# The last product of an FFN by a 7-for-8 algorithm, one factor of the weight at a time, on one Trainium2 core

## The chip, the core and the metric

The kernel runs on one core of a Trainium2 chip. Its engines have queues of their own and run side by side: TensorE (PE) multiplies 128-row tiles into PSUM banks, VectorE (DVE) and ScalarE (ACT) work on PSUM and SBUF, GpSimd (POOL) on SBUF, and SyncE (SP) issues all DMAs of this kernel. The metric is the time of one execution on the device in microseconds; lower is better.

## The reference

Attention over 8 batches, 12 heads, 448 tokens and head size 64, with q and k normalized, and then an FFN without activation: two products of the 3584 x 768 attention output with 768 x 1536 weights, multiplied elementwise, and a last product with a 1536 x 768 weight. The weights come as float64.

```python
q_n, k_n = (rmsnorm(q, g_q), rmsnorm(k, g_k))
scores = scale * np.matmul(q_n, k_n.transpose(0, 1, 3, 2))
attn = softmax(scores)                       # rows
x = np.matmul(attn, v) -> (3584, 768)
out = ((x @ w_a) * (x @ w_b) @ w_out).astype(np.float32)
```

## The kernel before

**Order by a planner.** Nearly every operation is given to a small planner, class Plan, with its engine, an estimated duration, a key, and what it reads and writes. The planner goes forward in estimated time; on each engine it takes, of the operations that could start first, the one with the smallest key. The order that it finds is written out: each engine then works through its list in that order, and waits in it. Durations on the chip don't change the order.

**Attention** runs over 48 pairs of heads (`p` = 0 to 47; six pairs per batch). Per pair: load q, k, v; squares, `ms` sums, a power on POOL (L428); `qn` (L432); transposes on TensorE (L461) and their copies to `qkT` (L466 on ACT, L470 on DVE); scores (L483) and exponentials (L489, ACT) in four chunks; the product with v (L504); sums over keys (L539), from the fourteenth pair on over chunks first added up on DVE and POOL (L517, L519); reciprocals (L557); the result to `x` (L574, L578). The first 12 pairs (`LEAD`) use another split among engines.

**The FFN** runs in four blocks (`beta` = 0 to 3) of two batches, 896 tokens, once their 12 pairs are through. Its operations have larger keys than attention's, so on TensorE it fills what attention leaves. The first two products (`quarter_products`, L657) already use an algorithm with 7 products in place of 8: 12 steps per block, each with one "factor" tile `st` of 7 sums of weight quarters, into two of the PSUM banks "mm", evacuated on DVE, ACT and POOL into `hT`; the evacuation `U` (L685, L687) is an early one of each step. Input tiles `x` are nine, of which a block uses seven, so attention can run ahead of a block by one batch only, and stands still until its products are through.

**The last product** (L625) is plain: 7 chunks of 128 tokens, 2 halves of 384 columns, 12 matmuls each with all of w_out in SBUF (`w_out_sb`), copied from PSUM on DVE (L635) and ACT (L637) and stored.

**The weights** are rounded from float64 in 36 pieces of 128 x 768: one operation on ACT (L258), five on DVE (L259, L260, L262, L264, L265), one on POOL (L267). For w_a and w_b, two pieces make a factor (three sums on DVE, one on POOL, L343), which is kept in DRAM (L349) for blocks 1 to 3 and loaded again there (`stream`). Three `st` buffers rotate over factors in the making and in use. The 12 pieces of w_out (`round_out`) go to `w_out_sb`, the first eight through the memory of `hT`, the last four through `st` buffers.

## Time and profile before

| | |
|---|---|
| time, median of 3 runs | 1730.97 us (1730.71 to 1731.92) |
| profiled execution | 1732.12 us, its span 1730.2 us |
| TensorE busy | 1650.3 us, 95% |
| DVE busy | 742.7 us, 43% |
| POOL, ACT busy | 543.1 us, 372.2 us |
| moved by DMA | 139.49 MB |

The profile is of one execution. Busy time is that in which an engine has at least one instruction at work. The rows of a group give line, engine, operation and shapes, count, busy us and mean ns of one, and behind the bar the idle time just before them. The rows of waits give who waited for whom, us in total, times and the longest. Rows of the timeline give start, duration, engine, line, count, and in brackets the idle time before and what ended it. Rows of windows give a stretch and the busy us and count of each engine in it.

### The profile page before, as it was taken

Reading aid. Unit: us, or ns where it says so; the run is one execution under the profiler, and the core shown is the slowest. Engines: PE = TensorE matmul, PEld = TensorE weight load, DVE = VectorE, ACT = ScalarE, POOL = GpSimd, SP = SyncE. Lnnn points to the kernel's source line nnn. Section 1 sums busy time; section 2 is a strip of 40 time slices with the busy share of each in tenths; the row PEclk is TensorE's granted clock in tenths of the full one; section 3 lists DMA queues with packets and bytes.
Section 4 is the critical chain, followed back from the end, with each engine's and each line's share of the span. In section 5 each row is a group of like instructions: output and inputs, shape, how many; then the busy total and the mean of one; then the engine's idle time right before and its main releaser. Section 6 shows DMA issues by size and latency. Waiting matters only on the chain. (4 is left out here: it accounts for less than half of the span.)

```text
span 1730.2 us, 14844 instructions
## 1 busy us (share of the span) xinstructions
PE 1650.3 (95%) x5616; PEld 803.3 (46%) x5616; DVE 742.7 (43%) x936; ACT 372.2 (22%) x666; POOL 543.1 (31%) x320
## 2 busy tenths in 40 slices
PE   5799799899889999999999999999999999999998
PEld 2333343344344444555444544455544555555554
DVE  8877687876644434222353534222253202222100
ACT  5676223221222223000132223100023000000000
POOL 4535556553544445010164444201042000010000
PEclk9899899999989999999999999999999999999999
DMA  8343133443331111222221111222220001220000
GB/s 285 110 119 97 49 125 129 158 145 120 108 106 50 51 47 47 96 96 75 90 77 49 51 46 49 77 96 73 86 91 20 23 28 64 96 95 32 14 28 25
DMA packets 104790, 139.49 MB, mean 81 GB/s; under 512 B 49924, under 2 KB 97028, under 8 KB 98564
## 3 DMA queue, kind: packets, MB, share of 16 engines
q1 hardware_dynamic: 104708, 138.44, 24.6%
q8 instruction: 46, 0.75, 0.2%
q14 instruction: 36, 0.29, 0.1%
HBM read 110.89 MB, written 27.53 MB: 80 GB/s over the span
## 5 line engine op out<-in xcount | busy, mean ns | idle before, releaser
L657 PE MATMUL pq<-x,st 128*128 128x448 f32 x2016 | 772.5, 542 | 12.3 <-DVE U L685 3.4
L657 PEld LDWEIGHTS pq<-x,st 128*128 128x128 f32 x2016 | 379.6, 190 | 395.4 <-issue 372.1
L625 PE MATMUL po<-w_out_sb,hT 128*128 128x384 f32 x1344 | 443.5, 488 | 0.0
L625 PEld LDWEIGHTS po<-w_out_sb,hT 128*128 128x128 f32 x1344 | 251.8, 190 | 182.7 <-issue 15.9
L489 ACT ACTIVATE ET<-sc,ms 112x448 f32<-112x448 f32 x384 | 212.8, 635 | 356.1 <-PE sc L483 294.8
L519 POOL TENSOR_TENSOR sum<-sum,ET 112x896 f32<-112x896 f32 x72 | 159.5, 2215 | 334.4 <-DVE sum L517 331.9
L483 PE MATMUL sc<-qkT 64*112 64x448 f32 x768 | 176.9, 581 | 32.3 <-DVE qkT L470 30.9
L557 DVE RECIPROCAL su<-su 128x224 f32<-128x224 f32 x72 | 112.7, 1565 | 165.1 <-PE su L539 164.1
L704 POOL TENSOR_TENSOR hT<-hT,t 128x448 f32<-128x448 f32 x24 | 27.2, 1132 | 475.6 <-DVE t L703 475.6
L504 PE MATMUL o<-ET,v_sb 112*64 112x448 f32 x768 | 166.7, 556 | 0.0
L428 POOL TENSOR_TENSOR ms<-ms,expo 112x16 f32<-112x16 f32 x48 | 142.8, 2974 | 54.2 <-DVE ms L424 42.9
L483 PEld LDWEIGHTS sc<-qkT 64*112 64x112 f32 x768 | 63.2, 178 | 126.5 <-issue 97.0
L418 DVE TENSOR_REDUCE ms<-sq 112x8 f32<-112x512 f32 x96 | 65.3, 680 | 102.3 <-POOL sq L413 99.7
L504 PEld LDWEIGHTS o<-ET,v_sb 112*64 112x64 f32 x768 | 50.7, 139 | 105.5 <-issue 103.3
L635 DVE COPY o_sb<-po 128x384 f32<-128x384 f32 x28 | 15.6, 556 | 192.7 <-PE po L625 192.7
L637 ACT COPY o_sb<-po 128x384 f32<-128x384 f32 x28 | 13.4, 479 | 273.3 <-PE po L625 258.0
L715 POOL TENSOR_TENSOR hT<-hT,t 128x448 f32<-128x448 f32 x48 | 55.5, 1159 | 40.6 <-DVE t L713 40.6
L679 ACT COPY hT<-pq 128x448 f32<-128x448 f32 x24 | 12.8, 532 | 254.8 <-PE pq L657 254.8
L709 DVE TENSOR_TENSOR hT<-U,pq 128x448 f32<-128x448 f32 x48 | 29.8, 620 | 71.3 <-PE pq L657 71.3
L682 ACT COPY t<-pq 128x448 f32<-128x448 f32 x24 | 12.8, 532 | 210.1 <-PE pq L657 210.1
L267 POOL TENSOR_TENSOR st<-st,w_out_sb 128x768 f32<-128x768 f32 x18 | 34.0, 1887 | 68.5 <-DVE w_out_sb L265 49.7
L432 DVE TENSOR_TENSOR qn<-q_sb,ms 112x512 f32<-112x512 f32 x48 | 53.5, 1114 | 4.0 <-POOL ms L428 3.2
(70 smaller groups left out, 941.9 us busy)
## 6 DMA issues: line engine op xcount, KB each, us to landing
st<-kept SPq DMA_DIRECT2D x36, 1344.0 KB, 5.6
kept<-st SPq DMA_DIRECT2D x12, 1344.0 KB, 4.8
q_sb<-in_q_dram SPq DMA_DIRECT2D x48, 224.0 KB, 2.6
k_sb<-in_k_dram SPq DMA_DIRECT2D x96, 112.0 KB, 2.8
v_sb<-in_v_dram SPq DMA_DIRECT2D x48, 224.0 KB, 2.6
w_out_sb<-in_moe_w_b_dram SPq DMA_DIRECT2D x20, 384.0 KB, 3.9
hraw<-in_moe_w_out_dram SPq DMA_DIRECT2D x8, 768.0 KB, 5.1
w_out_sb<-in_moe_w_a_dram SPq DMA_DIRECT2D x16, 384.0 KB, 3.8
```

The costliest lines, as they stand in the source:

```text
L267: ("POOL", 2, step(lambda hi, hif, lo, lof, w, wb: nc.gpsimd.tensor_tensor(w, w, lof, ALU.add)), "x", "w"))
L418: nc.vector.tensor_reduce(rs[p][:, s], xs["sq", nm, p], AX, ALU.add)
L428: nc.gpsimd.tensor_tensor(msf, msf, expo, ALU.pow)
L432: nc.vector.tensor_tensor(qns[p].rearrange("p j h d -> p h j d"), xs["q", p].rearrange("p h (j d) -> p h j d", d=D), rs[p][:, 0].rearrange ...
L483: nc.tensor.matmul(t[:, e, 0:S], lhsT=qkTs[p][rows, 1, c * SP:(c + 1) * SP], rhs=qkTs[p][rows, 0, :], start=True, stop=True)
L489: nc.scalar.activation(E[:, e], scs[p, c][:, e, 0:S], AF.Exp, scale=rs[p][:, 1, 2 * c + e:2 * c + e + 1])
L504: nc.tensor.matmul(os_[p][e * D:(e + 1) * D, :], lhsT=xs["v", p][:, e, c * D:(c + 1) * D], rhs=ETs[p, c][:, e], start=(c == 0), stop=(c == ...
L519: nc.gpsimd.tensor_tensor(sums[p], sums[p], ETs[p, c], ALU.add)
L557: op("DVE", 1.55, p, lambda half=half: nc.vector.reciprocal(sus[p][:, half], sus[p][:, half]), [], [su])
L625: nc.tensor.matmul(held["po"][:, 0:HALF], lhsT=hTs[0][:, m].rearrange("p a s -> p (a s)")[:, t * P:(t + 1) * P], rhs=w_out_sb[:, m, x * HA ...
L657: nc.tensor.matmul(banks[bank][:, 0:S], lhsT=sts[at][:, f, c * P:(c + 1) * P], rhs=quads[x][:, c], start=(start and c == 0), stop=(stop an ...
L715: take("POOL", 1.15, lambda i=i, n=n, nm=nm: nc.gpsimd.tensor_tensor(C(i, n), C(i, n), held[nm], ALU.mult), [t], [hp[i]])
```

## The change

The last product now uses the 7-for-8 algorithm too. The two halves of the tokens and of the 12 row tiles of `hT` are one side, the quarters of w_out the other. A pair of 128-token chunks takes 7 products of 6 matmuls, each into its own PSUM bank; sums of `hT` chunks are formed on DVE, partly in place, and the products are added up on the way out of PSUM, seven adds on DVE and one copy on ACT per pair. A block has 7 chunks, so the odd one of an even block is set aside (`left`) and paired with that of the next block: 3 pairs in blocks 0 and 2, 4 in blocks 1 and 3. The loop runs factor by factor over all pairs, and each factor (1180 KB, all six tiles of its k) comes from DRAM into an `st` buffer.

w_out is therefore not held in SBUF. Its 12 pieces become 6 factors (numbers 12 to 17), made like the others and kept in DRAM. Factors are made in the order `seq`, three of w_out first; a factor's weight loads wait for the scores of a pair given by `GATES`. The normalization of a pair has a smaller key (`p - 4.0` for `p - 1.5`).

```diff
+        NORM = 4.0
...
-        def factors(n):
+        def factors(n, key, early, after):
...
+            if last:
+                m = n - len(order)
+                steps = ((0, 4, 1, 0), (0, 5, 3, 1), (1, 1, 3, 4), (0, 6, 2, 1))
...
+                words, row = place(early)
...
+                    if last:
+                        k = m + part * MH
+                        nc.sync.dma_start(words(), moe_w_out[k * P:(k + 1) * P, :])
+                        return
...
+                op("SP", 0.5 if last else 1.0, key - 2.5, load, after, [row], kb=768)
...
+                    nc.sync.dma_start(kept["o"][:, :, m], sts[n])
...
-        def round_out(kc):
...
-            ms, key = tile_of(f"ms{p}", "ms", 3), p - 1.5
+            ms, key = tile_of(f"ms{p}", "ms", 3), p - NORM
...
-            seven = 2 * S // P
-            for t in range(seven):
-                for x in range(2):
...
-                                nc.tensor.matmul(held["po"][:, 0:HALF],
-                                                 lhsT=hTs[0][:, m].rearrange("p a s -> p (a s)")[:, t * P:(t + 1) * P],
-                                                 rhs=w_out_sb[:, m, x * HALF:(x + 1) * HALF],
-                                                 start=(m == 0), stop=(m == KO - 1))
...
+            def sum_(to, x, y, alu):
+                op("DVE", 0.98, -0.5, lambda: nc.vector.tensor_tensor(to[0](), x[0](), y[0](), alu), x[1] + y[1], to[1][:1])
...
+            def product(t, f, a, take):
...
+                        for c in ks:
+                            nc.tensor.matmul(held["po"][:, 0:HALF], lhsT=a[0]()[:, c], rhs=sts[beta, 12 + place_of[f]][:, c],
+                                             start=(c == 0), stop=(c == MH - 1))
...
+            for f in (0, 1, 2, 4, 3, 5, 6):
+                stream(beta, 12 + place_of[f], f)
+            for t in pairs:
+                sum_(n_(t), A(1, 0, t), A(1, 1, t), ALU.add)
+                sum_(n_(t), n_(t), A(0, 0, t), ALU.subtract)
+            for t in pairs:
+                product(t, 0, A(0, 0, t), lambda po, ps, t=t: op(
+                    "ACT", 0.5, -1, lambda: nc.scalar.copy(acc(t, 0), ps()), [po], [c_(t)]))
+                sum_(A(0, 0, t), A(0, 0, t), A(1, 0, t), ALU.subtract)
+            for t in pairs:
+                product(t, 1, n_(t), lambda po, ps, t=t: op(
+                    "DVE", 0.6, -1, lambda: nc.vector.tensor_tensor(acc(t, 1), acc(t, 0), ps(), ALU.add), [po, c_(t)], [U_(t)]))
+            for t in pairs:
+                product(t, 2, A(0, 1, t), out_(t, 0, 0, 0))
+                sum_(A(0, 1, t), A(0, 1, t), n_(t), ALU.subtract)
+                sum_(n_(t), A(1, 0, t), A(1, 1, t), ALU.add)
...
+                product(t, 5, A(0, 0, t), both)
+            for t in pairs:
+                product(t, 6, A(1, 1, t), out_(t, 1, 0, 1))
+            if not odd:
+                op("ACT", 1.5, 0, lambda: nc.scalar.copy(left(), H()[:, :, 2 * OWN * P:]), allh, [f"{fin}/left"])
...
-        for n in range(len(order)):
-            factors(n)
-        for kc in range(KO):
-            round_out(kc)
+        GATES = [0, 0, 1, 3, 5, 7, 8, 10, 11, 11] + [12] * 8
+        seq = [12, 13, 14, 0, 1, 2, 3, 4, 15, 5, 6, 16, 7, 8, 9, 17, 10, 11]
         for p in range(NP + 1):
+            for x, n in enumerate(seq):
+                if p == GATES[x]:
+                    factors(n, x * 1.1 + 0.5, x < 6, [f"scored{p - 1}"] if p else [])
```

How the lists move, at three places. Rows name the line, the operation, and tiles as out<-in; a row of TensorE counts matmuls in the program, each of which is two instructions in the trace.

TensorE, at the end of block 0's twelve steps (`pq`) and the start of its last product (`po`), before:

```order
L657 MATMUL pq<-x,st 128x448 x3
L483 MATMUL sc<-qkT 112x448 x4
L539 MATMUL su<-sum,ones 64x448 x2
L504 MATMUL o<-ET,v_sb 64x448 x4
L461 MATMUL pt<-ident,k_sb 128x112 x4
L461 MATMUL pt<-ident,qn 128x112 x4
L625 MATMUL po<-w_out_sb,hT 128x384 x6
L483 MATMUL sc<-qkT 112x448 x4
```

and now:

```order
L741 MATMUL pq<-x,st 128x448 x6
L496 MATMUL sc<-qkT 112x448 x4
L552 MATMUL su<-sum,ones 64x448 x2
L517 MATMUL o<-ET,v_sb 64x448 x4
L474 MATMUL pt<-ident,k_sb 128x112 x4
L474 MATMUL pt<-ident,qn 128x112 x4
L741 MATMUL pq<-x,st 128x448 x3
L669 MATMUL po<-st,hT 128x384 x18
L669 MATMUL po<-st,fin 128x384 x3
L496 MATMUL sc<-qkT 112x448 x4
```

After a pair's transposes stood 6 matmuls of the last product, and then the next scores; now 3 of the last step, 18 of the first factor with chunks of `hT` and 3 of the second with a sum (`fin`) stand between them.

DVE at the same place, before (from a pair's reciprocals to the `qkT` that these scores read):

```order
L557 RECIPROCAL su<-su 128x224 x2
L578 TENSOR_TENSOR x<-x,su 128x448
L517 TENSOR_TENSOR sum<-ET 112x896
L259 TENSOR_SCALAR w_out_sb<-w_out_sb 128x768
L260 TENSOR_SCALAR w_out_sb<-w_out_sb 128x768
L262 SCALAR_TENSOR_TENSOR w_out_sb<-st,w_out_sb 128x768
L264 TENSOR_SCALAR st<-w_out_sb 128x768
L265 SCALAR_TENSOR_TENSOR st<-st 128x768
...
L432 TENSOR_TENSOR qn<-q_sb,ms 112x2x4x64
L470 TENSOR_SCALAR qkT<-pt,gain 128x448
```

(the marked gap is a second rounding, the same five rows) and now:

```order
L570 RECIPROCAL su<-su 128x224 x2
L445 TENSOR_TENSOR qn<-q_sb,ms 112x2x4x64
L591 TENSOR_TENSOR x<-x,su 128x448
L431 TENSOR_REDUCE ms<-sq 112x8
L797 TENSOR_TENSOR t_2651<-U,pq 128x448
L530 TENSOR_TENSOR sum<-ET 112x896
L657 TENSOR_TENSOR fin<-hT 128x768
L657 TENSOR_TENSOR fin<-fin,hT 128x768
...
L657 TENSOR_TENSOR hT<-hT 128x6x128 x2
L431 TENSOR_REDUCE ms<-sq 112x8
L437 TENSOR_SCALAR ms<-ms 112x16
L483 TENSOR_SCALAR qkT<-pt,gain 128x448
```

(the gap holds the same two sums for the second and third pair of chunks). Two roundings of w_out are gone from this place, `qn` stands right behind the reciprocals, and eight sums of `hT` chunks stand ahead of `qkT`.

DVE in the stretch of block 0 in which its steps run without attention, one step from `U` to `U`, before:

```order
L685 TENSOR_TENSOR U<-hT,pq 128x448
L259 TENSOR_SCALAR st<-st 128x768
...
L695 TENSOR_TENSOR hT<-U,pq 128x448
L343 TENSOR_TENSOR st<-st 128x384
L701 TENSOR_TENSOR hT<-hT,pq 128x448
L343 TENSOR_TENSOR st<-st 128x384 x2
L709 TENSOR_TENSOR hT<-U,pq 128x448 x2
L259 TENSOR_SCALAR st<-st 128x768
...
L687 TENSOR_TENSOR U<-t_2335,pq 128x448
```

and now:

```order
L769 TENSOR_TENSOR U<-hT,pq 128x448
...
L261 TENSOR_SCALAR st<-st 128x768
...
L779 TENSOR_TENSOR hT<-U,pq 128x448
L365 TENSOR_TENSOR st<-st 128x384 x2
L785 TENSOR_TENSOR hT<-hT,pq 128x448
...
L261 TENSOR_SCALAR st<-st 128x768
...
L793 TENSOR_TENSOR hT<-U,pq 128x448
...
L261 TENSOR_SCALAR st<-st 128x768
...
L771 TENSOR_TENSOR U<-t_2351,pq 128x448
```

(behind each L259 or L261 stand the other four operations of its rounding, in part among the evacuations). Two roundings stood in a step; now three begin in this one, and pieces of w_out are among them.

More of the change, by code (lines that the diff above doesn't have):

```diff
@@ L214 @@
     small = const.tile([1, 1], I32, name="small")
-    w_out_sb = const.tile([P, KO, DM], FP32, name="w_out_sb")
     grow = const.tile([1, 2, D], FP32, name="grow")
@@ L271 @@
     NB = B // 2
-    WE = 8
+    OWN = 2 * S // P // 2
+    PAIRS = OWN + 1
+    assert 2 * S == (2 * OWN + 1) * P and NB % 2 == 0
     def fast():
@@ L716, in quarter_products, with store @@
                          [t], [hp[i]])
-        def store(beta, t, x, o_sb):
-            g, end = 2 * S * beta + t * P, 2 * S * beta + (t + 1) * P
+        def store(g, x, o_sb):
+            end = g + P
             at = 0
@@ L790, in general @@
                             step[2]()
+            w_out_sb = ws.pop()
             ps = pool("g_ps", 2, space=PSUM)
```

165 lines of the change are left out of this document (101 added, 64 removed).

## The prediction

> **What bounds the kernel now.** First the page: how busy is TensorE, and where not.
>
> ```profile
> PE 1650.3 (95%) x5616; PEld 803.3 (46%) x5616; DVE 742.7 (43%) x936; ACT 372.2 (22%) x666; POOL 543.1 (31%) x320
> PE   5799799899889999999999999999999999999998
> PEclk9899899999989999999999999999999999999999
> ```
>
> TensorE is busy 1650.3 of 1730.2 us, so 79.9 us of the span are open, and by the 40 slices (43.3 us each) nearly all of them lie in the first twelve, before 520 us. There the product of two numbers decides: a matmul count times the rate at which matmuls start. Second, therefore, the rate, from stretches that hold nothing else: the windows of the last product's line alone, and of the first two products' line alone.
>
> ```profile
> 1350.00:1400.00 50.00, 50.00 (x157) 29.46 (x156) 1.00 0.09 24
> 1450.00:1500.00 50.00, 50.00 (x134) 25.27 (x133) 1.00 0.23 83
> L625 PE MATMUL po<-w_out_sb,hT 128*128 128x384 f32 x1344 | 443.5, 488 | 0.0
> ```
>
> 157 instructions of 384 columns in 50 us are 0.3185 us each; 134 of 448 columns are 0.373 us. The mean of 488 ns in the group's row is a latency and not a price, since neighbours overlap. Third, all engines by stage. The cuts are my own: 193, 358 and 424.5 us are the DVE evacuations "U" (lines 685 and 687) in the first, seventh and eleventh of the twelve steps of the first FFN block, 487 us is where its last product runs freely.
>
> ```profile
> 40.00:115.00 75.00, 65.36 (x336) 25.80 (x335) 59.73 (x79) 50.78 (x93) 35.98 (x14) 0.93 0.40 127
> 115.00:170.00 55.00, 53.62 (x283) 20.87 (x283) 43.41 (x53) 36.44 (x66) 25.45 (x14) 1.00 0.37 107
> 170.00:193.00 23.00, 14.02 (x42) 5.58 (x40) 19.44 (x18) 5.29 (x10) 11.65 (x6) 0.68 0.16 45
> 192.97:358.07 165.10, 154.47 (x529) 66.90 (x526) 132.14 (x160) 48.45 (x83) 97.71 (x58) 0.99 0.36 118
> 358.07:424.50 66.43, 63.76 (x165) 30.37 (x164) 51.89 (x70) 8.47 (x12) 27.11 (x18) 1.00 0.45 157
> 424.50:487.00 62.50, 50.21 (x173) 22.82 (x172) 39.86 (x49) 15.54 (x27) 28.84 (x16) 0.89 0.31 110
> 487.00:690.00 203.00, 203.00 (x799) 98.97 (x798) 86.91 (x104) 58.87 (x109) 93.86 (x52) 1.00 0.20 56
> ```
>
> Columns: stretch, length, then busy us (and count) of PE, PEld, DVE, ACT, POOL, then granted clock, DMA share, GB/s. From 487 us TensorE has no gap while DVE and POOL are under half busy: fewer matmuls there are time, one for one. From 193 to 424.5 us DVE is 78 to 80% busy in an order written out beforehand, and TensorE loses 2.7 to 10.6 us per stage: there DVE is nearly the bound. Fourth, what TensorE waits for, over the whole span (the first four rows), from 450 to 500 us, and from 487 us to the end.
>
> ```profile
> PE sc L483 <- DVE qkT L470: 30.9, 13, 12.3
> PE pt L461 <- DVE qn L432: 17.3, 3, 8.9
> PE pt L461 <- DMA k_sb<-in_k_dram: 9.8, 1, 9.8
> PE pq L657 <- DVE x L592: 3.3, 1, 3.3
> ...
> PE sc L483 <- DVE qkT L470: 12.3, 1, 12.3
> ...
> PE sc L483 <- DVE qkT L470: 7.2, 5, 1.4
> ```
>
> Nearly all waits are for DVE, and after 487 us they are only 7.2 us. The longest one is this:
>
> ```profile
> 460.01 1.76 PE L483 MATMUL sc<-qkT 64*112 64x448 f32 x8
> 462.73 3.17 DVE L557 RECIPROCAL su<-su 128x224 f32<-128x224 f32 x2 [1.15 <-PE su L539]
> 464.94 4.05 PE L625 MATMUL po<-w_out_sb,hT 128*128 128x384 f32 x12
> 467.79 4.57 POOL L519 TENSOR_TENSOR sum<-sum,ET 112x896 f32<-112x896 f32 x2 [1.86 <-DVE sum L517]
> 468.13 2.31 DVE L260 TENSOR_SCALAR w_out_sb<-w_out_sb 128x768 uint32<-128x768 uint32 x1
> 470.47 2.71 DVE L262 SCALAR_TENSOR_TENSOR w_out_sb<-st,w_out_sb 128x768 uint32<-128x768 uint32 x1
> 479.84 0.69 DVE L432 TENSOR_TENSOR qn<-q_sb,ms 112x512 f32<-112x512 f32 x1
> 481.27 3.33 PE L483 MATMUL sc<-qkT 64*112 64x448 f32 x8 [12.29 <-DVE qkT L470]
> ```
>
> The last two roundings of w_out stand in DVE's queue ahead of the qn and qkT that the next scores need. TensorE idles 12.29 us, and its next eight score instructions take 3.33 us where the eight before took 1.76.
>
> **The change, part by part.**
>
> *The last product.* Two blocks of 896 tokens are 14 chunks, 7 pairs; a pair takes 7 factors x 6 matmuls = 42 where two chunks took 2 x 2 x 12 = 48. Four blocks: 14 pairs x 42 = 588 in place of 672, and each is two instructions in the trace (672 are its x1344). 168 instructions fewer, x 0.3185 = **-53.5 us**, in stages where TensorE had hardly a gap. An even block now has 3 pairs (252 instructions) in place of 336, an odd one keeps 336: the saving falls in blocks 0 and 2.
>
> *What DVE gets for it.* Per pair five sums of 128x768 and seven evacuations that add (two banks' worth of copies went before, half of them on ACT). Neither sum is in the trace; the rows around it:
>
> ```profile
> L635 DVE COPY o_sb<-po 128x384 f32<-128x384 f32 x28 | 15.6, 556 | 192.7 <-PE po L625 192.7
> L517 DVE TENSOR_TENSOR sum<-ET 112x896 f32<-112x896 f32 x36 | 39.1, 1085 | 0.0
> L343 DVE TENSOR_TENSOR st<-st 128x384 f32<-128x384 f32 x36 | 24.8, 689 | 7.5 <-POOL st L267 5.7 <-POOL st L343 1.4
> L703 DVE TENSOR_TENSOR t<-t,pq 128x448 f32<-128x448 f32 x24 | 14.9, 619 | 30.8 <-PE pq L657 30.8
> ```
>
> A sum lies between 0.69 (384 elements) and 1.09 us (896); I take 0.95. An add from PSUM costs at most the 0.62 us of 448 elements. Block 0: 15 x 0.95 + 21 x 0.62 less 7 copies of 0.56 = 23 us; block 1: 20 x 0.95 + 28 x 0.62 - 4 = 32 us. In the 203 us from 487 us DVE has 116 us free, and TensorE's work there shrinks by 27 us: 110 of 176 us busy, 62%, less than the 80% at which TensorE lost 10.6 of 165 us above. So hidden in the main, but not wholly, since a bank is now evacuated every 12 instructions (3.8 us) and not every 24: **+5 us** over the mixed stages, between 0 and 27 (the upper end is priced under the rivals). In block 3, without attention, DVE has per product 3.8 us for 0.6 to 1.2 us of adds: nothing. After the last matmul one add stands in place of one copy: nothing.
>
> What such a sum can meet, in the trace:
>
> ```profile
> 315.38 4.56 POOL L519 TENSOR_TENSOR sum<-sum,ET 112x896 f32<-112x896 f32 x2 [3.37 <-DVE sum L517]
> 315.66 2.35 DVE L432 TENSOR_TENSOR qn<-q_sb,ms 112x512 f32<-112x512 f32 x1
> 317.93 0.61 DVE L701 TENSOR_TENSOR hT<-hT,pq 128x448 f32<-128x448 f32 x1
> ```
>
> Two operands from SBUF, begun while POOL adds up: 2.35 us in place of 0.69. One operand from PSUM, with POOL still at work: 0.61 us as always. The Trainium skill (SBUF — State Buffer, Who interferes with whom) has the rule: a VectorE instruction with two SBUF inputs and a GpSimd one that reads SBUF exclude each other for the whole instruction. It speaks against this change, whose 70 sums are all of that kind, and these two rows agree with it.
>
> *The factors.* Now w_out's 12 chunks make 6 factors that are rounded in st buffers, combined (3 DVE operations, 1 POOL) and written to DRAM. The count of roundings stays 36. Price of one on DVE, five operations:
>
> ```profile
> L259 DVE TENSOR_SCALAR st<-st 128x768 f32<-128x768 f32 x24 | 21.5, 895 | 9.2 <-ACT st L258 9.0
> L260 DVE TENSOR_SCALAR st<-st 128x768 uint32<-128x768 uint32 x24 | 26.3, 1094 | 0.8
> L262 DVE SCALAR_TENSOR_TENSOR st<-w_out_sb,st 128x768 uint32<-128x768 uint32 x18 | 19.8, 1098 | 0.6
> L264 DVE TENSOR_SCALAR w_out_sb<-st 128x768 uint32<-128x768 uint32 x18 | 10.1, 562 | 0.6
> L265 DVE SCALAR_TENSOR_TENSOR w_out_sb<-w_out_sb 128x768 f32<-128x768 uint32 x18 | 17.3, 960 | 0.6
> ```
>
> 0.895 + 1.094 + 1.098 + 0.562 + 0.960 = 4.6 us. The order of DVE gives the counts between the same evacuations, before and now:
> - to the first U (193 us): 14 roundings and 9 combinations become 12 and 18: -9.2 + 6.2 = -3 us of DVE. They also move: by the seventh pair's reciprocals 10 have become 12 and none follow, so pairs 1 to 6 may wait for DVE (two more roundings at most, +9 us), while the third qn comes 17 DVE rows sooner (up to -8.9 us of the start's waits). From 170 to 193 us TensorE works 14 of 23 us at a clock of 0.68: behind the combinations (3.3 us of wait) a rounding stood ahead of qkT, now none does; I count -7 of these 9 us and +2 for the pairs: **-5**, between -17 and +9.
> - 193 to 358 us, products mixed with attention: 11 and 15 become 13 and 18: +11.3 us of DVE into 33 free; at that load some of it shows: **+5**, between 0 and 11.
> - 358 to 424.5 us, products alone: 7 and 12 become 11 and 15: 4 x 4.6 + 3 x 0.69 = 20.5 us of DVE into 66.43 - 51.89 = 14.5 free: at least +6, at most +20.5; midway, **+13**. The w_out factors also take one st buffer of three each in turn, so the next FFN factor is begun a step later.
> - 424.5 to 487 us: the roundings ahead of qkT are gone, and with them 12.3 us and the slow restart (3.33 less 1.76 us): **-14**. In their place stand eight sums (7.6 us) ahead of a qkT, but behind 36 + 6 matmul instructions (13.4 us) that cover them; if they don't, -4.
>
> *The DMAs.* 28 loads of 1180 KB from DRAM, 6 writes of 1344 KB.
>
> ```profile
> st<-kept SPq DMA_DIRECT2D x36, 1344.0 KB, 5.6
> ```
>
> A load lands in at most 5.6 us; its buffer's predecessor is in use for 3 pairs x 12 x 0.3185 = 11.5 us or more, and three buffers rotate: nothing. The weight loads that now wait on SP for scores hold up q, k and v of pairs two ahead, and a pair takes some 11 us there (283 instructions in 55 us, 56 a pair): nothing; uncovered it would be the 9.8 us of the start's k wait, once.
>
> Sum: -53.5 + 5 - 5 + 5 + 13 - 14 = **-49.5 us**. The profiled execution took 1732.12 us (span 1730.2): 1682.6. The median of the runs is 1.1 us lower: **1681 us**.
>
> **The rivals.**
>
> *FFN block 0 becomes bound by DVE.* All upper ends from the start to 424.5 us: +9 + 11 + 20.5 where I counted +13; 27 us more: 1708. For it: 78 to 80% busy in a fixed order. Against: half of that order's idle time was before the very roundings that leave it.
>
> *The sums are held up by POOL in all mixed stages.* Each of some 45 sums under attention costs 0.95 + 1.66 us (2.35 - 0.69); from 487 us DVE is then 110 + 25 = 135 of 176 us busy, 77%, near the load at which TensorE lost 6.4% of 165 us; 6.4% of some 420 us of mixed stages (176 in block 0, some 190 in block 1, the rest in block 2) is 27 us in place of my 5: 1703. Against: POOL is under half busy there and most DVE work reads PSUM.
>
> *The early relief comes whole.* -17, 0, +6, -14 early and 0 late: 1653. For it: all waits in the first 500 us were on a DVE order that no longer stands.
>
> *Slower: two PSUM banks are too few.* A product fills its bank in 3.8 us; if its evacuation stands behind a pair of reciprocals (3.17 us) and a held sum (2.35 us), TensorE waits 1.7 us. Of 98 products some 57 run under attention: +97 us in place of my 5, 1773. It decides from some 0.95 us a product on (54 / 57). For it: half the matmuls per bank. Against: in the mixed stage from 193 us six steps fill 24 banks, of 6 to 18 instructions, and TensorE lost 10.6 us, 0.4 us each; at that price it is the 25 us of the rival before.
>
> *The change doesn't do what it says:* if attention's own chain, not TensorE, held the mixed stages, only the part of block 2 that runs without attention would gain, some 20 us: 1711. The 203 of 203 us speak against it.
>
> **How the numbers follow.** My forecast 0.60 (its own range 1665 to 1697), DVE-bound block 0.14, held sums 0.08, early relief 0.12, two banks 0.04, no filler 0.02. The time is the forecast's, 1681; the range takes in most of the relief and of the DVE-bound cases: 1656 to 1707. A difference of 0.2% (3.5 us) is what a measurement can tell here. Slower is the case of the two banks, 0.04; 0.01 is left for a time within the 0.2%; faster 0.95.
>
> **What would show it.** Right: 588 x 2 instructions in the last product, 157 of them per 50 us in block 3; the 12.3 us wait for qkT gone; TensorE without gaps from the first last product on; the four early stages at about 188, 170, 79 and 48 us. Wrong: waits of the last product for DVE of over 20 us in total (banks or sums); TensorE gaps in the steps 7 to 11 beyond 20 us; or the span's saving other than the 53 us less matmuls by more than the early stages show.

## The result, and the profile after

| | before | changed |
|---|---|---|
| time, median | 1731.45 us (1730.71 to 1733.18) | 1692.64 us (1690.15 to 1695.11) |
| ratio, 95% interval | | 0.9774 (0.9757 to 0.9791) |
| span of the profiled execution | 1730.2 us | 1692.0 us |

The change is 2.3% faster. The forecast was 1681 us, 11.6 us too low; its range (1656 to 1707) holds the time. The page of the changed kernel, busy time and the slices:

```profile
PE 1606.0 (95%) x5448; PEld 774.1 (46%) x5448; DVE 891.9 (53%) x1094; ACT 365.9 (22%) x654; POOL 571.1 (34%) x326
PE   5989889988999999999999999999999999999998
```

TensorE is busy 44.3 us less than before (1650.3), and the open part of its span is 86.0 us in place of 79.9: of the work that was saved, some came back as waiting. DVE has 149 us more to do. The windows: the first two are cut at the same times as in the prediction, the next ones at the same places of the program (the first, seventh and eleventh "U" are now at 186.49, 355.56 and 443.03 us), and the last is a stretch of block 3's last product:

```profile
40.00:115.00 75.00, 68.36 (x346) 25.38 (x342) 70.20 (x89) 50.45 (x94) 37.16 (x17) 0.98 0.61 192
115.00:170.00 55.00, 48.99 (x248) 18.66 (x248) 36.97 (x45) 31.42 (x59) 25.26 (x15) 0.97 0.50 157
170.00:186.49 16.49, 10.70 (x38) 4.61 (x36) 14.52 (x13) 3.81 (x7) 7.34 (x5) 0.88 0.15 39
186.49:355.56 169.07, 156.49 (x518) 69.69 (x519) 138.91 (x165) 48.91 (x83) 96.83 (x55) 0.94 0.39 130
355.56:443.03 87.47, 74.28 (x190) 34.14 (x188) 82.73 (x99) 14.00 (x20) 47.64 (x27) 0.96 0.43 158
443.03:505.00 61.97, 58.60 (x200) 27.78 (x201) 37.52 (x44) 15.39 (x27) 27.90 (x15) 0.97 0.29 99
505.00:690.00 185.00, 181.59 (x704) 86.13 (x703) 104.46 (x124) 51.49 (x94) 89.06 (x47) 1.00 0.33 104
1600.00:1650.00 50.00, 50.00 (x157) 29.46 (x156) 14.52 (x21) 0.00 (x0) 0.00 (x0) 1.00 0.28 95
```

Two rows carry what follows. From 355.56 to 443.03 us DVE is busy 82.73 of 87.47 us, and TensorE is open for 13.2 us: this stretch is DVE's. From 505 to 690 us TensorE is now open for 3.4 us, where before it had no gap. In block 3 the rate of the last product is 157 instructions in 50 us, as before. Its groups, and the waits of TensorE over the whole span:

```profile
L669 PE MATMUL po<-st,hT 128*128 128x384 f32 x744 | 246.2, 487 | 0.0
L669 PE MATMUL po<-st,fin 128*128 128x384 f32 x432 | 145.3, 489 | 0.0
```

```profile
PE sc L496 <- DVE qkT L483: 19.5, 11, 3.4
PE pt L474 <- DMA k_sb<-in_k_dram: 8.7, 1, 8.7
PE pq L741 <- DVE U L769: 8.6, 4, 2.4
PE pt L474 <- DVE qn L445: 8.5, 2, 7.4
PE sc L496 <- ACT qkT L481: 7.7, 4, 3.2
PE pq L741 <- DVE t L782: 5.5, 2, 3.9
```

744 + 432 = 1176 = 588 x 2 instructions, and the idle time before them is 0.0. The longest wait for qkT is 3.4 us, not 12.3. The waits of the first products (L741) for evacuations on DVE have grown: 8.6 us for the first U of a step, where the same row had 3.4 us before. In the next table the span is cut at the start of the "U" of seven steps in each kernel's timeline (U0 is the first step of block 0, U6 its seventh; U10 its eleventh; U15, U26 and U36 lie in blocks 1, 2 and 3), us per stage:

| stage | before | changed | moved by | forecast |
|---|---|---|---|---|
| start to U0 | 193.0 | 186.5 | -6.5 | -5 |
| U0 to U6 | 165.1 | 169.1 | +4.0 | +5 |
| U6 to U10 | 66.5 | 87.5 | **+21.0** | +13 |
| U10 to U15 | 304.5 | 269.9 | -34.6 | |
| U15 to U26 | 389.4 | 394.6 | +5.2 | |
| U26 to U36 | 310.4 | 284.8 | -25.6 | |
| U36 to the end | 301.3 | 299.7 | -1.6 | |
| U10 to the end, sum | 1305.6 | 1249.0 | **-56.6** | -62.5 |

(The last forecast is -53.5 - 14 + 5.) So the miss is 8 us between U6 and U10 and 6 us after U10, less 2.5 us before U6. The experiments go after these two, and after what stands behind the two stages that came out as forecast.

### The profile page after: what moved, and what is told of

Read it like the earlier page. It is cut to its first block, busy times and chain, and to the rows that moved or that the text cites. A ratio compares the mean times of both kernels' runs of the same rounds, so it can differ in the third digit from the quotient of the medians.

```text
span 1692.0 us, 14761 instructions
## 1 busy us (share of the span) xinstructions
PE 1606.0 (95%) x5448; PEld 774.1 (46%) x5448; DVE 891.9 (53%) x1094; ACT 365.9 (22%) x654; POOL 571.1 (34%) x326
## 4 chain that ended last, share of the span: by engine, by line
PE 72%; DVE 20%; issue 3%; POOL 3%; DMA 1%; ACT 0%; SPq 0%; DVEq 0%; POOLq 0%; ACTq 0%
PE pq L741 37%; PE po L669 18%; PE sc L496 7%; PE o L517 6%; PE su L552 2%; DVE fin L657 2%; DVE st L261 2%; DVE st L262 2%; DVE st L264 2%; PE pt L474 1%; DVE su L570 1%; DVE sum L570 1%; DVE ms L431 1%; DVE st L365 1%; DVE lraw L267 1%
## 5 line engine op out<-in xcount | busy, mean ns | idle before, releaser
L741 PE MATMUL pq<-x,st 128*128 128x448 f32 x2016 | 780.8, 547 | 29.0 <-DVE U L769 8.6
L741 PEld LDWEIGHTS pq<-x,st 128*128 128x128 f32 x2016 | 383.1, 192 | 414.2 <-issue 373.5
L669 PE MATMUL po<-st,hT 128*128 128x384 f32 x744 | 246.2, 487 | 0.0
L496 PE MATMUL sc<-qkT 64*112 64x448 f32 x768 | 178.4, 582 | 30.3 <-DVE qkT L483 19.5
L669 PEld LDWEIGHTS po<-st,hT 128*128 128x128 f32 x744 | 139.9, 190 | 100.6 <-issue 7.8
L532 POOL TENSOR_TENSOR sum<-sum,ET 112x896 f32<-112x896 f32 x72 | 158.8, 2205 | 35.1 <-DVE sum L530 34.1
L441 POOL TENSOR_TENSOR ms<-ms,expo 112x16 f32<-112x16 f32 x48 | 148.3, 3089 | 55.0 <-DVE ms L437 53.4
L788 POOL TENSOR_TENSOR hT<-hT,t 128x448 f32<-128x448 f32 x24 | 28.3, 1180 | 409.6 <-DVE t L787 409.6
L426 POOL TENSOR_TENSOR sq<-k_sb 112x512 f32<-112x512 f32 x36 | 49.4, 1372 | 330.1 <-DMA k_sb<-in_k_dram 205.7
L669 PE MATMUL po<-st,fin 128*128 128x384 f32 x432 | 145.3, 489 | 0.0
L669 PEld LDWEIGHTS po<-st,fin 128*128 128x128 f32 x432 | 80.6, 190 | 61.2 <-issue 8.8
L689 DVE TENSOR_TENSOR o_sb<-fin,po 128x384 f32<-128x384 f32 x56 | 31.0, 553 | 110.9 <-PE po L669 110.4
L431 DVE TENSOR_REDUCE ms<-sq 112x8 f32<-112x512 f32 x96 | 65.2, 679 | 13.6 <-POOL sq L426 13.5
L269 POOL TENSOR_TENSOR st<-st,lraw 128x768 f32<-128x768 f32 x24 | 47.5, 1978 | 66.7 <-DVE lraw L267 60.7
L797 DVE TENSOR_TENSOR t<-U,pq 128x448 f32<-128x448 f32 x48 | 29.7, 619 | 67.3 <-PE pq L741 67.3
```

The source lines that it names most:

```text
L269: ("POOL", 2, step(lambda hi, hif, lo, lof, w, wb: nc.gpsimd.tensor_tensor(w, w, lof, ALU.add)), "x", "w"))
L426: nc.gpsimd.tensor_tensor(t, flat, flat, ALU.mult)
L431: nc.vector.tensor_reduce(rs[p][:, s], xs["sq", nm, p], AX, ALU.add)
L441: nc.gpsimd.tensor_tensor(msf, msf, expo, ALU.pow)
L496: nc.tensor.matmul(t[:, e, 0:S], lhsT=qkTs[p][rows, 1, c * SP:(c + 1) * SP], rhs=qkTs[p][rows, 0, :], start=True, stop=True)
L532: nc.gpsimd.tensor_tensor(sums[p], sums[p], ETs[p, c], ALU.add)
```

## The experiments

All times are medians. The kernel before, run beside each group of experiments, had medians of 1731.07 to 1732.66 us; the changed kernel is taken at its 1692.64 us, so differences of under 2 us between two times are not read.

### 1. Fewer matmuls alone

Edit, in the kernel before: in blocks 0 and 2 each output takes 9 of its 12 matmuls. A quarter of the sum over k is left out there; all else stays, the planner makes its order anew.

```diff
-                        ms = range(part * KO // 2, (part + 1) * KO // 2)
+                        K9 = KO if beta % 2 else KO - 3
+                        ms = range(part * KO // 2, min((part + 1) * KO // 2, K9))
```

> The kernel before with 9 of 12 matmuls per product in blocks 0 and 2 of the last product (42 of 168 matmuls left out in each, the rest of the sum is missing from the output); nothing else is changed. It takes the same 168 instructions from TensorE as the change, without its sums, factors and gates. Theory (matmuls there are time one for one): 168 x 0.3185 = 53.5 us less, 1678 us. Rival (part of it comes back as waits for DVE and POOL once TensorE has less to fill with): 40 to 47 us less, 1684 to 1691.

Measured: 1667.58 us (1666.54 to 1668.32), ratio 0.9625 (0.9609 to 0.9641), 65 us less, 11 us more than the theory had. Between U15 and U36 the span is 26.9 us shorter, where 84 instructions fewer were priced at 84 x 0.3185 = 26.75 us: one for one. Between U10 and U15 it is 37.1 us shorter: 26.75 and 10 us more, since in the order that the planner found here the long wait for qkT is gone too (1.0 us from 424 to 520 us), though the last two roundings still stand ahead of qn and qkT on DVE. So the saving was priced rightly, and most of the hole would have closed without any move of the roundings.

### 2. The sums left out

Edit: no sum of `hT` chunks is formed; the products that would read one read a chunk of `hT` as it is. The result lacks these sums; the matmuls are as many.

```diff
             def sum_(to, x, y, alu):
-                op("DVE", 0.98, -0.5, lambda: nc.vector.tensor_tensor(to[0](), x[0](), y[0](), alu), x[1] + y[1], to[1][:1])
+                return
```

> The changed kernel without the 70 sums of hT chunks on DVE; the products that read them read a chunk of hT in their place (the sums are left out, so the output isn't the product). Theory (the sums, on DVE ahead of qkT and held by POOL, cost the mixed stages what they lost beyond the matmuls: 6 us from step 10 to step 15, 5 us in block 1's, 1 us in block 2's): 10 to 13 us less, 1680 to 1683. Rival (the 98 evacuations into 2 banks cost it): 0 to 3 us less.

Measured: 1673.28 us (1672.18 to 1675.65), ratio 0.9661 (0.9645 to 0.9677), 19.4 us below the changed kernel and more than the theory had. The stages until U10 stay within 1 us; U10 to U15 falls by 7.4, U15 to U26 by 9.0, U26 to U36 by 4.3 us, and the waits for qkT from 19.5 to 6.1 us. So the sums cost about 20 us, not 5.

### 3. The sums on a sixth of their columns, order unchanged

Leaving an operation out lets the planner write another order. Here every sum stays in its place and works on the first of six row tiles; the products that read a sum in `fin` take its one tile in place of all six. Five sixths of each sum are left out.

```diff
-                op("DVE", 0.98, -0.5, lambda: nc.vector.tensor_tensor(to[0](), x[0](), y[0](), alu), x[1] + y[1], to[1][:1])
+                op("DVE", 0.98, -0.5, lambda: nc.vector.tensor_tensor(to[0]()[:, 0], x[0]()[:, 0], y[0]()[:, 0], alu), x[1] + y[1], to[1][:1])
```

> The changed kernel with every engine's order kept; the 70 sums work on one of six row tiles, and the products that read a sum read that tile six times (five sixths of each sum are left out). Theory (it is the sums' time on DVE that the mixed stages pay): 14 to 20 us less than the change, 1673 to 1679, nearly all of it between steps 10 and 36. Rival (without the sums the planner had found a better order, and that was the gain): 0 to 8 us less.

Measured: 1674.77 us (1673.61 to 1676.93), ratio 0.9667 (0.9651 to 0.9683), 17.9 us less; waits for qkT 9.0 us. The order is the same, so it is the time that the sums take on DVE. Where that time goes shows in the changed kernel's timeline, at the start of block 0's last product:

```profile
483.71 10.48 PE L669 MATMUL po<-st,hT 128*128 128x384 f32 x32
485.37 1.78 DVE L657 TENSOR_TENSOR fin<-hT 128x768 f32<-128x768 f32 x1 [1.02 <-POOL hT L799]
486.30 5.54 POOL L532 TENSOR_TENSOR sum<-sum,ET 112x896 f32<-112x896 f32 x2
487.18 2.72 DVE L657 TENSOR_TENSOR fin<-fin,hT 128x768 f32<-128x768 f32 x1
489.82 2.83 DVE L657 TENSOR_TENSOR fin<-hT 128x768 f32<-128x768 f32 x1
492.69 0.96 DVE L657 TENSOR_TENSOR fin<-fin,hT 128x768 f32<-128x768 f32 x1
...
497.96 0.68 DVE L483 TENSOR_SCALAR qkT<-pt,gain 128x448 f32<-128x448 f32 x1
498.55 1.22 DVE L657 TENSOR_TENSOR hT<-hT 128x768 f32<-128x768 f32 x1
498.69 2.23 PE L496 MATMUL sc<-qkT 64*112 64x448 f32 x8 [2.56 <-DVE qkT L483]
```

A row of sums stands in DVE's list ahead of the next qkT. The ones that meet POOL's addition take 2.72 and 2.83 us, the next, with POOL idle, 0.96 us. Of the 70 sums in this trace 25 run while POOL is at work and take 2.05 us in the mean; the other 45 take 0.95. TensorE runs out of products and waits 2.56 us. The two largest groups of the 70 sums:

```profile
L657 DVE TENSOR_TENSOR fin<-hT 128x768 f32<-128x768 f32 x28 | 43.3, 1548 | 4.8 <-POOL hT L799 4.3
L657 DVE TENSOR_TENSOR fin<-fin,hT 128x768 f32<-128x768 f32 x14 | 19.0, 1354 | 3.3 <-PE po L669 2.9
```

Together with the other three groups (11.3, 15.5 and 4.6 us) the sums take 93.7 us, 1.34 us each.

### 4. Normalization less far ahead

```diff
-        NORM = 4.0
+        NORM = 1.5
```

> The changed kernel with the normalization's key back at p - 1.5; the rest stays. Theory (the 6.5 us that the change won before the first U come from normalizing earlier): the first U at 191 to 196 us, the time 3 to 8 us over the change. Rival (they come from the gates and from the roundings' new places): the first U within 2 us of 186.5, the time within 2 us.

Measured: 1688.12 us (1686.97 to 1688.71), ratio 0.974 (0.9724 to 0.9757), 4.5 us faster than the changed kernel. My theory, that early normalization had brought the early gain, falls: the first U comes at 185.0 us, before 186.5.

### 5. The weight loads not paced

The changed kernel without the waits of the weight loads for attention's scores:

```diff
-                    factors(n, x * 1.1 + 0.5, x < 6, [f"scored{p - 1}"] if p else [])
+                    factors(n, x * 1.1 + 0.5, x < 6, [])
```

> The changed kernel without the waits of the weight loads for attention's scores. If the pacing costs or gains nothing, as the prediction says: 1691 to 1694 us, first U within 2 us of 186.5. If it is what brought the first U forward by 6.5 us: the loads of w_out's chunks and of the first factors crowd q, k and v of the first pairs, first U at 190 to 195 us, and the time 1696 to 1702 us. If the waits on the load queue held up the factors between the first and eleventh U: 1685 to 1690 us.

Measured: 1714.48 us (1712.03 to 1715.97), ratio 0.9905 (0.9888 to 0.9921), 22 us slower than with the pacing. The whole loss lies before the first U (208.35 us, against 186.5); later stages are within 2 us. The stretch from 20 to 60 us, of the changed kernel, then without pacing, and from that second run the first row of TensorE's waits over the span:

```profile
20.00:60.00 40.00, 37.34 (x192) 14.09 (x188) 38.59 (x50) 27.08 (x51) 23.17 (x11) 1.00 0.66 211
```

```profile
20.00:60.00 40.00, 21.75 (x96) 8.37 (x93) 34.20 (x42) 16.29 (x28) 19.25 (x11) 0.81 1.04 364
```

```profile
PE pt L474 <- DVE qn L445: 38.7, 4, 16.8
```

Without pacing the 16 DMA engines are full, TensorE does half as much, and once it waits 16.8 us for a qn. The weights come first and q, k and v of the first pairs after them. The second theory had the direction and the place; its price (4 to 10 us) was less than half of what was lost. The planner's order differs somewhat between the two kernels as well, on TensorE among the first pairs and on DVE.

### 6. One factor of w_out made earlier

Rounding that falls between U6 and U10 is moved ahead: the factor numbered 15 goes to the front of the sequence, three loads are released one pair sooner. Nothing is left out.

```diff
-        GATES = [0, 0, 1, 3, 5, 7, 8, 10, 11, 11] + [12] * 8
-        seq = [12, 13, 14, 0, 1, 2, 3, 4, 15, 5, 6, 16, 7, 8, 9, 17, 10, 11]
+        GATES = [0, 0, 1, 3, 5, 6, 8, 9, 11, 11] + [12] * 8
+        seq = [12, 13, 14, 15, 0, 1, 2, 3, 4, 5, 6, 16, 7, 8, 9, 17, 10, 11]
...
-                    factors(n, x * 1.1 + 0.5, x < 6, [f"scored{p - 1}"] if p else [])
+                    factors(n, x * 1.1 + 0.5, x < 7, [f"scored{p - 1}"] if p else [])
```

> The changed kernel with the fourth w_out factor (number 15) made right behind the first three, during the first 12 pairs, and not between FFN factors 4 and 5. Theory (steps 6 to 10 of block 0 are held by DVE's roundings): two roundings and three combinations, 2 x 4.6 + 3 x 0.69 = 11 us of DVE, leave the stretch from the first U to the eleventh; the first pairs have 20 us of DVE free and take them at a cost of 0 to 6 us: 5 to 11 us less than the change, 1682 to 1688. Rival (the early stage is as full): the same time as the change, or up to 5 us more.

Measured: 1683.33 us (1682.6 to 1685.12), ratio 0.9716 (0.97 to 0.9732), 9.3 us less. U6 to U10 takes 77.4 us in place of 87.5, the start 3.1 us more, U0 to U6 3.0 us less. DVE is busy 71.44 us from U6 to U10 in place of 82.73: DVE's work fills most of the stretch in both and sets its length, as the prediction said. The count of roundings is not all of that. One fewer begins there (10 for 11), each takes 4.94 us in place of 5.37, and attention's operations that had fallen into the stretch are out of it.

### 7. Fewer operations in these roundings

For the last three factors of w_out three of the five DVE operations of a rounding are skipped (L262, L264 and L261: clamp, shift and merge are left out, so the weights aren't rounded).

```diff
             for step, (e, n, emit, r, wr) in enumerate(round_steps(get)):
+                if bare and step in (1, 2, 3):
+                    continue
```

> The changed kernel in which the three w_out factors made inside block 0 (numbers 15 to 17) skip three of the five DVE operations of their roundings (those operations are left out, so the weights are not rounded there); buffers, loads, combinations and order of factors stay. 6 x (0.895 + 1.094 + 1.098) = 18.5 us of DVE less, about 12 of them between steps 6 and 10. Theory (DVE's work holds that stretch): it falls from 87.5 us to about 76, the time by 10 to 18 us, to 1675 to 1683. Rival (three st buffers, one of them taken by a w_out factor, hold it): the stretch stays above 83 us, the time within 5 us of the change.

Measured: 1690.39 us (1687.74 to 1692.03), ratio 0.9754 (0.9738 to 0.977). U6 to U10 falls to 76.3 us as expected, but U0 to U6 takes 5.3 us and the start 2.7 us more, in an order that the planner made anew. Inconclusive for the time: it mixes the cost of the operations with another order.

### 8. The same operations on 16 of 768 columns, order unchanged

```diff
+            part = lambda: tuple(a[:, 0:16] for a in get())
+            less = round_steps(part)
...
+                if thin and step in (1, 2, 3):
+                    emit = less[step][2]
```

The weights of these three factors are rounded in 16 of 768 columns only.

> The changed kernel with every engine's order kept; the three DVE operations that the run before left out of factors 15 to 17 now work on 16 of 768 columns (the other columns of those weights aren't rounded). Theory (DVE's work holds the steps of block 0; the run before gave its 11 us back because the planner, told of less work, wrote another order for the steps before): step 6 to 10 again near 76 us, steps 0 to 6 at 163 to 169, the time 11 to 17 us under the change, 1676 to 1682. Rival (work taken from DVE there only lets TensorE wait elsewhere): within 5 us of the change.

Measured: 1682.12 us (1681.21 to 1682.74), ratio 0.9707 (0.9691 to 0.9724), 10.5 us less, but U6 to U10 only 3.1 us shorter, at 84.4, where skipping the same operations had taken 11 us off it; U0 to U6 is 7.0 us shorter, and the start 1.6 us longer. DVE is still busy 80.79 us from U6 to U10, against 82.73, so most of what was taken from its operations there came back. The timeline of this run shows how:

```profile
395.11 0.17 DVE L261 TENSOR_SCALAR st<-st 128x16 f32<-128x16 f32 x1
395.27 1.83 POOL L269 TENSOR_TENSOR st<-st,lraw 128x768 f32<-128x768 f32 x1 [3.49 <-DVE st L261]
395.31 1.83 DVE L262 TENSOR_SCALAR st<-st 128x16 uint32<-128x16 uint32 x1
397.17 0.17 DVE L264 SCALAR_TENSOR_TENSOR st<-lraw,st 128x16 uint32<-128x16 uint32 x1
```

An operation on 16 columns takes 0.17 us, and 1.83 us if it begins just after POOL's addition of the rounding before: it ends 0.04 us after POOL does. In the changed kernel the same pair stands like this:

```profile
395.50 1.83 POOL L269 TENSOR_TENSOR st<-st,lraw 128x768 f32<-128x768 f32 x1 [1.25 <-PE pq L741]
395.57 2.18 DVE L262 TENSOR_SCALAR st<-st 128x768 uint32<-128x768 uint32 x1
397.78 0.96 DVE L264 SCALAR_TENSOR_TENSOR st<-lraw,st 128x768 uint32<-128x768 uint32 x1
```

This gave the next theory: POOL's addition, the last operation of a rounding, holds DVE in the first operations of the rounding after it.

### 9. POOL's addition on 16 of 768 columns

In all roundings; no DVE operation is touched. The weights lack their low part in the other columns.

```diff
+            less = round_steps(lambda: tuple(a[:, 0:16] for a in get()))
+            for step, (e, n, emit, r, wr) in enumerate(round_steps(get)):
+                if e == "POOL":
+                    emit = less[step][2]
```

> The changed kernel in its own order; POOL's addition in each rounding of a weight (line 269) works on 16 of 768 columns, so the weights lack most of their low part. No instruction of DVE is changed or left out. Theory 'POOL holds DVE': in the 11 rounded pieces between the seventh and the eleventh U, DVE's operations on SBUF were stretched while POOL added (a 16-column operation took 1.83 us), so the stretch falls from 87.5 to 72 to 78 us, the one before it from 169 to 160 to 165 us, and the time to 1668 to 1678 us. Rival 'DVE's own work': nothing on DVE is shortened, so the stretch stays within 3 us of 87.5 and the time at 1688 to 1693 us. Third way: the chain of one piece is shorter without 2 us of POOL, but only the last piece before a factor gains by it: 1685 to 1690 us.

Measured: 1644.54 us (1643.2 to 1645.71), ratio 0.9495 (0.948 to 0.9511), 48 us less than the changed kernel, about twice what the theory had. Start to U0 174.3 us (-12.2), U0 to U6 152.6 (-16.4), U6 to U10 71.8 (-15.7), the rest within 5 us in sum. The groups of DVE from U6 to U10, in the kernel before (358.07 to 424.55 us; its lines L259, L260 and L262 are L261, L262 and L264 of the changed kernel):

```profile
L259 DVE TENSOR_SCALAR st<-st 128x768 f32<-128x768 f32 x7 | 9.8, 1405 | 0.8 <-ACT st L258 0.7
L260 DVE TENSOR_SCALAR st<-st 128x768 uint32<-128x768 uint32 x7 | 4.7, 676 | 0.2
L262 DVE SCALAR_TENSOR_TENSOR st<-w_out_sb,st 128x768 uint32<-128x768 uint32 x7 | 6.7, 959 | 0.2
```

the changed kernel (355.6 to 443 us):

```profile
L262 DVE TENSOR_SCALAR st<-st 128x768 uint32<-128x768 uint32 x11 | 16.8, 1528 | 0.3
L264 DVE SCALAR_TENSOR_TENSOR st<-lraw,st 128x768 uint32<-128x768 uint32 x11 | 13.6, 1240 | 0.3
L267 DVE SCALAR_TENSOR_TENSOR lraw<-lraw 128x768 f32<-128x768 uint32 x11 | 11.3, 1029 | 0.2
L261 DVE TENSOR_SCALAR st<-st 128x768 f32<-128x768 f32 x11 | 11.2, 1017 | 0.0
L266 DVE TENSOR_SCALAR lraw<-st 128x768 uint32<-128x768 uint32 x11 | 6.1, 557 | 0.2
```

and with the thin addition (327 to 399 us):

```profile
L264 DVE SCALAR_TENSOR_TENSOR st<-lraw,st 128x768 uint32<-128x768 uint32 x11 | 12.1, 1103 | 0.3
L267 DVE SCALAR_TENSOR_TENSOR lraw<-lraw 128x768 f32<-128x768 uint32 x11 | 11.3, 1031 | 0.2
L261 DVE TENSOR_SCALAR st<-st 128x768 f32<-128x768 f32 x11 | 8.9, 810 | 0.0
L262 DVE TENSOR_SCALAR st<-st 128x768 uint32<-128x768 uint32 x11 | 8.3, 756 | 0.3
L266 DVE TENSOR_SCALAR lraw<-st 128x768 uint32<-128x768 uint32 x11 | 6.1, 558 | 0.2
```

The sums of the five means per rounding: before 4.56 us (with 0.56 and 0.96 us for the last two), changed 5.37, thin addition 4.26. L262 falls by half, though nothing of it was changed; the operations that run while POOL has nothing to add (L266, L267) stay within 2 ns. So POOL's addition does hold DVE, 1.1 us per rounding here. The windows row of this stretch, and the page's busy times:

```profile
326.94:398.75 71.81, 68.82 (x185) 33.16 (x184) 69.64 (x98) 14.08 (x20) 29.79 (x27) 0.98 0.53 193
PE 1590.4 (97%) x5448; PEld 771.8 (47%) x5448; DVE 846.1 (51%) x1094; ACT 366.9 (22%) x654; POOL 514.5 (31%) x326
```

From U6 to U10 DVE is busy 69.64 us in place of 82.73 and still sets the stretch: 13.1 of its 15.7 us are DVE's busy time. Over the whole run that time falls by 45.8 us (891.9 to 846.1), every engine's order being the same: the five operations take 4.07 us in place of 4.90 in the mean of the 36 roundings, 30 us in sum, and other operations of DVE that had met the additions are shorter too. The addition itself is also a link in the chain of a factor (1.98 us on POOL, 0.39 us thin); what that adds to the 48 us was not separated.

### 10. Better versions: late sums, and the addition on DVE

Two edits that leave nothing out. First, on top of experiment 6, the sums get a key that lets attention's operations go first:

```diff
-                op("DVE", 0.98, -0.5, lambda: nc.vector.tensor_tensor(to[0](), x[0](), y[0](), alu), x[1] + y[1], to[1][:1])
+                op("DVE", 0.98, 60.0, lambda: nc.vector.tensor_tensor(to[0](), x[0](), y[0](), alu), x[1] + y[1], to[1][:1])
```

> The run with factor 15 made early, and the key of the sums raised from -0.5 to 60, behind attention's operations on DVE and ahead of the FFN's. Theory (sums ahead of qkT are what TensorE waits for): its waits for qkT fall from 20 to under 8 us and the time by 5 to 12 us from 1683, to 1671 to 1678. Rival (sums put off hold up the second factor's products instead): 1683 or more, with waits of the last product's matmuls for the sums.

Measured: 1676.74 us (1676.52 to 1678.31), ratio 0.9676 (0.966 to 0.9693), 6.6 us below experiment 6; the waits for qkT fall from 20.5 to 10.1 us (the theory had under 8), and one new wait of 4.0 us of the last product for a sum appears. About a third of the sums' 20 us is only a matter of order.

Second, on top of that, the rounding's last addition goes from POOL to DVE:

```diff
-            ("POOL", 2, step(lambda hi, hif, lo, lof, w, wb: nc.gpsimd.tensor_tensor(w, w, lof, ALU.add)), "x", "w"))
+            ("DVE", 2, step(lambda hi, hif, lo, lof, w, wb: V.tensor_tensor(w, w, lof, ALU.add)), "x", "w"))
```

> The version with reordered factors and late sums (1676.7 us), and in it the rounding's last addition moved from POOL to DVE, for all 36 pieces; the result is complete. Theory 'POOL holds DVE': DVE gets some 0.95 us more per piece and loses stretches of 1.4 us and more and the hand-over to POOL and back; 3 to 12 us less: 1665 to 1674 us. Rival 'DVE's own work': DVE is 91 to 95% busy between the seventh and the eleventh U, so 11 times 0.95 us more there is paid in full and some of it in the stretch before: 1685 to 1692 us.

Measured: 1668.64 us (1668.14 to 1670.43), ratio 0.9636 (0.962 to 0.9652), 8.1 us less, as the theory had. The page's busy times, with late sums and then with the addition on DVE as well, and the additions from U6 to U10 (339.4 to 427.1 us):

```profile
PE 1603.7 (96%) x5448; PEld 773.4 (46%) x5448; DVE 881.9 (53%) x1094; ACT 365.3 (22%) x654; POOL 570.4 (34%) x326
PE 1599.1 (96%) x5448; PEld 773.0 (46%) x5448; DVE 885.1 (53%) x1130; ACT 366.2 (22%) x654; POOL 500.3 (30%) x290
L269 DVE TENSOR_TENSOR st<-st,lraw 128x768 f32<-128x768 f32 x11 | 11.9, 1078 | 0.2
```

DVE has 36 more operations of about 1 us each, and its busy time rises by 3.2 us only: the holds that went with POOL's additions cost it nearly as much as the additions do. That speaks against the rival, but it doesn't make up the 8.1 us, since DVE has no less to do in all. The hand-over to POOL and back is gone too, and the planner wrote another order; which of these gave the time was not tested. The gain lies before U6 (4.5 us to U0 and 13.7 us from there). U6 to U10 takes 87.6 us again, 10.4 more than with late sums alone; part of that is attention's work that now falls into it: TensorE is busy 78.3 us there, against 69.6.

Last, the normalization's key of experiment 4 on top of this version:

> The version before (reordered factors, late sums, all of the rounding on DVE; 1668.6 us) with the normalization's key back at 1.5 pairs ahead. If the gains add: 1668.6 less the 4.5 us that this key was worth in the changed kernel, 1662 to 1666 us, and above all the waits of TensorE for ACT in the first 190 us fall while those for qn rise. If the key's worth came from the order that POOL's additions made, nothing is left: 1667 to 1671 us.

Measured: 1699.85 us (1699.19 to 1702.62), ratio 0.9816 (0.98 to 0.9832): 31 us slower than without it, where 4 us less was hoped for. The first U comes at 203.2 us in place of 184.5, U0 to U6 takes 166.5 us in place of 154.9, and the waits for qn have grown from 6.4 us, once, to

```profile
PE pt L474 <- DVE qn L445: 28.4, 8, 6.4
```

A key that gained in the changed kernel loses in this one, which differs from it by three edits (an early factor, late sums, the addition on DVE). Which of them turns it, and why, was not tried. The best complete version is the one before, 1668.64 us, 24 us below the changed kernel.

## Why the prediction was right in the whole and wrong in its parts

**The products, -53.5 us: right.** 1176 instructions, 157 of them in 50 us, no idle time before them, and experiment 1 gives 26.9 us for a forecast 26.75.

**To the first U, -5 us: right in size (-6.5), wrong in its parts, and so in part by luck.** The pacing was costed at nothing: "uncovered it would be the 9.8 us of the start's k wait, once". In fact the stage hangs on it: without it the first U comes 21.9 us later than with it and 15 us later than before the change (the planner's order differs a little there too). The step looked only at what the waiting loads hold up on SP's queue, not at what the loads of w_out, now first in the sequence, would do to q, k and v if they didn't wait. The gain from freed DVE work that I put in the sum is not shown by any run, and the earlier normalization gained nothing: with the old key the first U comes at 185.0 us and the time is 4.5 us lower (experiment 4).

**193 to 358 us, +5 us: right in size (+4.0), its working not tested.** DVE's busy time rose by 6.8 us (132.14 to 138.91), where 11.3 us of work were counted.

**358 to 424.5 us, +13 us: mis-sized, +21.0.** The step that failed is the price of a rounding, 4.6 us, multiplied by the four that are added. It was added up from the means of five groups over the whole span before, and it holds for the seven of before in this stretch (4.56 us). With eleven in a row the next rounding begins while POOL adds for the last one, and each of the eleven takes 5.37 us, by experiment 9 because POOL holds DVE. DVE's busy time here rose by 30.8 us (51.89 to 82.73) where 20.5 us were counted; 9.8 us of it were covered, where +13 needs 7.5. So the work was under-priced, not the cover over-priced: 11 x 0.81 us = 8.9 us are the price, and some operations of attention's last pair before the pause, which were earlier before, fall into the stretch as well (DVE's L530 and L431, 1.4 us each, and POOL's L532 and L441); I had not counted these. The upper bound of the prediction (20.5 us, all DVE work uncovered) had the same price in it and was passed. In this stretch the "DVE-bound block" came true; in the two before it did not.

The hold stood in the prediction's own rows. L260 at 468.13 us took 2.31 us and L262 behind it 2.71 us, beside POOL's L519; the medians of these lines in the kernel before are 0.56 and 0.96 us. I read the rows for their order alone.

The prediction quoted the Trainium skill (SBUF — State Buffer, Who interferes with whom) for the sums alone, with the half of its rule that speaks of two SBUF inputs. The same section of the Trainium skill also has VectorE operations in a two-port performance mode excluded by GpSimd. L262 has one input, and the rows above (1.53 us, and 0.76 us without POOL's addition; 1.83 us for 16 columns) agree with that half, though no run shows the mode in which L262 works. I had applied neither half to the roundings.

**424.5 to 487 us, -14 us: right in the main.** The wait of 12.3 us for qkT has become one of 2.6 us. The clause "eight sums ahead of a qkT, but behind 13.4 us of matmuls that cover them" did not quite hold: three held sums (1.78, 2.72, 2.83 us for 0.95 each) used the cover up. Experiment 1 shows that the hole would also have closed mostly with the saved matmuls alone.

**Mixed stages, +5 us: mis-sized.** From U10 on the span moved by -56.6 us; with -53.5 and -14 that leaves +10.9. The sums alone cost 19.4 us (experiment 2), so about 8 us of relief stand against them that I did not foresee and whose source no run shows. The step that failed is the price of a sum: 0.95 us is its median with POOL idle, the mean is 1.34. The rival "held sums" named this mechanism, with 0.95 + 1.66 us for one and 27 us in all; the prediction gave it 0.08 and set its own term with the unheld price, though the row with 2.35 us was quoted there. Experiment 10 adds that the sums' place in the order is worth 6.6 us of it.

**Two PSUM banks too few: not so.** No wait of the last product for a bank appears in the list of waits. **Early relief whole: not so**, U6 to U10 alone speaks against it. **DMAs, nothing: right** for the streamed factors (28 loads, 5.2 us to land, no wait of TensorE for one); the 5.6 us that the prediction calls the most a load takes is a median.

What stays open: why the normalization's key gains 4.5 us in one order and loses 31 in another, what the shorter chain adds to the hold in experiment 9, what gave the 8.1 us of the addition on DVE, and the 8 us of relief after U10.

## What to carry to other kernels

When an edit packs more VectorE work next to GpSimd work on SBUF, price each operation by its mean in the densest stretch of the trace, not over the span, and compare that mean with its shortest; a run with GpSimd's operation cut short tells whether the difference is a hold. An operation moved from GpSimd to a full VectorE can be nearly free there: 36 additions of about 1 us added 3.2 us to VectorE's busy time here. And when weight loads are moved to the front, look at the queue that feeds the first stage: without the pacing this kernel was 22 us slower.

## What the runs showed of the hardware that I had not expected

A VectorE operation with one input, on 16 columns, took 1.83 us in place of 0.17 when it began 0.04 us after a GpSimd addition of 1.83 us on SBUF; on 768 columns the same operation took 2.18 us in place of 0.56 (its line's median in the changed kernel). It ended 0.04 us (16 columns) and 0.42 us (768 columns) after the GpSimd operation did. With the 36 additions cut to 16 columns VectorE's busy time fell by 45.8 us and the time by 48 us; with the complete additions on VectorE the time fell by 8.1 us.
